# A new written order for all steps, and two kinds of rounding taken from VectorE and given to ScalarE alone

## The chip, the cores and the metric

One Trainium2 chip, one core. The metric is the device time of one execution in microseconds (us); lower is better. Engines are named as in the profile: PE is TensorE's matmul, PEld its weight load, DVE is VectorE, ACT is ScalarE, POOL is GpSimd, SP is SyncE, which here issues all DMAs.

## The reference

Attention over pooled queries, followed by a two-layer MLP, all in float32:

```python
q_pool = q.reshape(B, H, S // 2, 2, D).mean(axis=3)          # B=4, H=8, S=1152, D=64
scores = scale * np.matmul(q_pool, k.transpose(0, 1, 3, 2))
attn = np.exp(scores - scores.max(-1)) ; attn = attn / attn.sum(-1)
x = np.matmul(attn, v)  ->  [2304 tokens, 512]
h = x @ w_in                                                  # [2304, 2048]
out = np.maximum(0.01 * h, h) @ w_out                         # [2304, 512]
```

## The kernel before

The work is cut into 3557 steps. There are 32 heads (4 batches of 8) and 9 token blocks of 256 for the MLP. Each operand of a precise matmul is split into a rounded high part and the rest, its low part, and three products of the parts are summed in PSUM. For keys these are `k_hi` and `k_lo`, for queries `q_hi` and `q_lo`, for an MLP block's input `x_hi` and `x_lo`, for the activations between the layers `post` 1 and `post` 2.

A head runs through these steps. `load_k`, `load_q`, `load_v` bring its inputs; `k_tr` and `q_tr` transpose on PE; `qk` (L465, L468) computes scores once to find each row's maximum, which DVE reduces straight from PSUM (`vmax`, L480); `m_tr`, `m_cp` (ACT) and `m_dma` (two DMAs, L500) lay the negated maxima out as one row of a matmul operand, `mt`; `qkt` (L515, nine tiles t) computes the scores again, transposed and less the maximum; `exp` (ACT, L519) writes a tile to SBUF; `esum` (POOL, L529) adds tiles up; `pv` (PE, L541) multiplies by V; `r_mm` sums over keys, a short chain of small DMAs inverts that sum and spreads it, `norm` and `scale` finish the head, and `x_out` writes it to DRAM.

An MLP block i waits for the heads that it needs, then `x_load` (SP) brings its input from DRAM, `x_hi` rounds it, `x_lo` (POOL, L675) takes the rest, and `l1` (L695) multiplies by w_in tiles that `ws_load` fetches again and again (512 KB each). Blocks 0 to 3 go on with `post` 0 (ACT, L703, the leaky ReLU), `post` 1 (rounding to the high part, helper line L259), `post` 2 (POOL, L708, the low part) and `l2` (L827 to L829). Blocks 4 to 8 use a seven-product scheme for the second layer (`g_act`, `g_mix`, `g_hi`, `g_lo`, `l2s` at L786, `o_mix`). Blocks 0 to 3 are interleaved with the heads; blocks 4 to 8 come mostly after them.

What sets the order: `ORDER` is a string of 3557 characters; each character is a letter for one of 65 families of steps (`FAMILIES`, `LETTERS`), and stands for that family's next step. `Scheduler.run` goes through it and issues each step in turn, so the string fixes the order of instructions in every engine's own queue. Where a step's `eng` names two engines, the planner picks the one that by its own books finishes it first; `lock=True` marks, in these books, a step that DVE and POOL may not run at the same time. Every engine takes its queue strictly in order, so a step that waits holds back all that are written behind it on the same engine.

Of the kernel before, what the change touches and what calls it, by code (L numbers as in the profile page):

```python
# [43 lines left out]
)  # L44
LETTERS = "!#$%&()*+,-./0123456789:;<=>?@ABCDEFGHIJKLMNOPQRSTUVWXYZ[]^_`abcd"
ORDER = (
    "!@(!#$)*%(++!,+#,+,B,$---%)*...-.--...+(+A-,-/)01*.&!-++.2.-,3,34-(,4.-34#5.AA..33$4A-%B34/01.53--442.53344#)B"
    ".$(33%-.4B4--*+,6+,.33..!CDC4D4E&/E63AAB4&34B-)355805412.34-37-54.*B.+(,-+,AA!63344.#$5%3-69B.)4:-B8../3434-0."
    "-13-..55&4573!3-9;.54555-434234*3+3.44,+,7#<=:-$.#$A./B%%63F-.->.;4F96?0GG1834&-5(33.-44.<3-5&)5342553-44.=3C."
    "!C4H34.D6C*DAEFE+3>4DE#:+,,GH3$/63CF5%CD;4EFGGC344!DE7DE01(A-A<9?H.--.63.434-=2334&433!>B):44.F#*+8-;6+,.,$535"  # L50
    "553%GCH?44-384(3A.!.</B4-3-..46)0*-1-DA6E.=.(23H++,,-4-F>7.FA..934/35-)3?8-.434&34BB5554.-0-1A3.3445555G55.-#$"
    ".C7(93%-..4233:;*44++G3B3:D6A,&,/0<F4G455;<134E3-4CDF.G34)-6B!3.-.43E5#B-243$=>=>7%.455C3*4+AD3E+-4-,B9?,C6.8!"
    "C..A-FDDGE/E.36FF40-B3.(1:-H.5F73494?34;5-32U38)-&43.&-...43<4435#43:$3;45*G/345%01(3C6++,D,CEGDE=A4B6>35442A)"
    "?85345-.*++33<,,#4UA=$-.6(34A-47935.-46%>)!-?FHRF8G.34.3-../-45&5-3.S743.G(394--..T4*G5H:+B,CBV;:&<VVVVBDV0#1+"
    "C!625WED-,-55FEF6=$X.)..%/3;3U4G4G#3$%37A>0434A91A34(4-.3H344-3*?52++643,4,34.5U-65<5Y354.U:;3-H8=3.44>73CCDED"
    "E5BVVVVVVVVU4<--9FW?G.F..XC8/!DVVVVGC30WA1HH4EDE63344=-23>43.-A)343B55X.55YY?546344348-*UU#+$VU.VVV+:%,,VUVW--"
    ".-VVV.&5555VV.!V3A./0W4155X-3B3B4.#2-.YBB63F43$%CD44-E6U-GC.FF34-GDE7..93344;&-34.53.54G/3HCD05ZCDEFE4ZZFFZZZZ"
    "B5GGCZHZZZHG1XCCCDEZ[ZAVZYFG:HDDUUZEE5DFGE3F2VGZ[VUVVVVVVVVVFW43W;5(5)<<B6CDX34G4=BE*+>?,F3+,35U584643345YA473"
    "-GCVXU=>V9V(D:VEVF.ZV;ZZW?ZY4ZZ8&A3<-=G-X.YZZZZZ&)4.--..-.ZZZ!.U[>/UZZ*01+U+,,6355555[2R5#S3?4T434$%68A33-7A43"
    "4943.-.-.VVVV4-.-(.-..&UU:5VVVVVVWV3/55X)*++UU0!15VVV;55WVVV,XUYYVVVV<W4Z34#,Z$%(VXVVWAX-3-.4ZZYY-..=23-ZZZZ55"  # L60
    "[U796U34.4)>*+,&A?:334;<+555645,=3-3844-A334.>3..(/04)71?546!69823344#ZZZZ$-:;<%.5555-.-.&!ZZZA=Z-3]]5.[>55-43"
    "43*VVVV+,.V?V+-4()3WA,43..47/012343#XUU*U4++,5,555$%633449-53.63555-48U3.4-43AA.344-3-VV:VV(VVV!YVVVV.;55U-U)W"
    "...XY554<VWXYVVVVVVWXY(=>UUU/ZZZZ034ZZZ12Z6&3?[3744RST334#*9:$6]43%)-++,,;55555<=8.3-4VVVU>UVVV4Z55WZ-!-X..-VV"
    ".ZVZVV3.-4#..34VZZZZ$/&%&[0AAA?-W6.132!-.4337-4.43(Y-.6-4U8X3.9:35555544-U5533..*/04;431Y+2,3+76,4<54334#)&*=>"
    "++4AU6,,VVVVVV9$W5?8VVVVVVW3%-A3-44A:&X.334-4355554.-Z-..!-;55.ZZ.YZZX().3/05#$1Y4UUZU2!5ZZ[-3-%.465.34555-3.4"
    "<73-=.9>U-6.3-4:343445;?.<3.*4/8=0A134+2346635555+43749(3A344,>?,)A*348#+3+:,!,$V%4VVV-U.-.;-.VZZ(VWZU55-.-.VV"
    "VVA-5#$3X%5U55Y!ZV4VZ..5/--0ZWAVVVV1.UVZV342.-.<-=)>Z.[XW364-.3U4374]93344(#3*5+555$+,6,&)%75U4?:YA!98334&4--;"
    "<XY3V.V4./VZ-.0551:#3VVV2Z5WXZYZZZZZ43U;.R555-$%64[34=<>=5.-3433.4(-.]*55++,,6>4-?S3434555T&../70833A1A-2A4)63"
    "49:4.;?3-63438<44-.3-434.5.5534--*+V..(5=,+!),VVVV.VWX7>?9&33/:0;416555468233#44*(+3$%+A,AZ,ZZ4-3.<55-.VZVYVU4"
    "3--.&AZU5UUZ-43ZZ.VV4V[5-W..34555553!45#.3$/01%UVVVVV4V2673W34!#43I)I$=3>4%96XXYY34?8-5543-555..:;U3443-43*V+V"  # L70
    "VVVVWVVV5+Z,,UV.4-UUU--..LVNOZ5VXWX..YM/ZZAZZZ01ZZZ<P[55QJ2KIIPQAZZZ=ZZLZ3674-34[363.&9-4>?:3445&8.-33-..4MA34"
    "-VV;-.4.VV.5YVVWX3/0U5VV515V55NVVUVVVVUV5YWXY42JVVW36434363<KO43I447XU339=4U4>R57933YS46UT546NVZIVJVPK::;;<<U5"
    "O55?VLVVVVMZ555V=QIU^VVVV>UUVVVVUUZIPZQVV5VV?Z8ZZVVZNVVJ7LI8IO^LJMZUUUVVVVVVVVVP[ZZZZZMNZZ_KKIRUUUN^VV9UQ_`VVV"
    "V`OVVaa^IV^S_VU:bbO^PTVVVV__JI`aLUVVVUVVVI[V^_bUVVMUK;QNIVVVV`a^]VV]IJJKKbLM<LMNOO`UPPVQVVUVVVUVVVab`a_`b^UVa^"
    "^UUV==VVV>>QUV^VVVVVbV_`UVVabbb^__b`a`V^c??ccUVUcVVRVVVUbcccVVaVcSbU^UVTVV^_`aUUVVVVVVVVV^_U__UUVb`VVVVVVaVb^U"
    "UUVVddVVUU__VV`Va_Vb`VVRaVVVb^`a^VVV`bUVVVabccbcbb_cUUVVVUVVVVSccccT`UUVVV^Va_^b^`_U_a_VVVVUVVVVV_^b`a^UVVVUVV"
    "VVb`UaVUV^VVUVUbVVU`VVVVabV`U`aaVV^VVVVUVVVd_RdSbb`ab^^bbccTccccbUVVVUUVVUUc__`a`VVVVaVVVVVc^b^U^UUVVVVVUU__VV"
    "Vb___VVV`aVVV`b`VVaUUVba`aU^VVVVVV^UVVVVbVd`dbabUVVV^UVV_`UVVV_`aa^bbbcc^]c_bccUUVVVVVccd`VaVbb___`a`ab`ab^_^_"
    "^_`bab`abcd`abbbbbbbbbbbbbccccccccddd"
)  # L80
TILINGS = {"pv": 1, "r_mm": 2, "qk": 3, "qkt": 3, "k_tr": 3, "q_tr": 3, "m_tr": 3}

# [134 lines left out]
def tile_pooled_attention_moe(  # L217
# [16 lines left out]
    B, H, S, D = q.shape  # L234
# [6 lines left out]
    KC = DM // 128  # L241
    NF = DFF // 128
    NB = 256
# [466 lines left out]
    S1, S2, S3, S4, A12, A22, A11, A21 = range(8)  # L710
# [158 lines left out]
    def step(fn, *a, eng, lat=None, deps=(), order=(), takes=(), lock=False):  # L869
        sch.add((fn.__name__, *a), partial(fn, *a), eng, lat, [d for d in deps if d], [d for d in order if d], takes, lock)  # L870
# [9 lines left out]
    for hd in range(NHD):  # L880
# [93 lines left out]

    for i in range(NBLK):
        step(x_load, i, **sp(1 + (i * NB // SP != (i * NB + NB - 1) // SP), 0.524e6), deps=[("x_out", hd) for hd in needs(i)] + [("x_load", i - 1) if i else None], takes=[("xb", [("l1", i, FH - 1 if i >= FAST else NF - 1, 2)])])
        step(x_hi, i, eng={"ACT": act(KC * NB), "DVE": dve(KC * NB, 2)}, lock=True, deps=[("x_load", i)])
        step(x_lo, i, eng=pool(KC * NB, "x_lo"), lock=True, deps=[("x_hi", i)])
        fast = i >= FAST
        order = [x * FH + p for p in range(FH) for x in (1, 0)] if fast else list(range(NF))  # L980
        for at, f in enumerate(order):
            (fp, _), hf = pair(i, f), f // FH
            was = order[at - 1] if at else NF - 1 if i <= FAST else FH - 1
            prev = ("l1", i, was, 2) if at else ("l1", i - 1, was, 2) if i else None
            step(ws_load, i, f, **sp(1, 0.524e6, 0.36), deps=[("w_out_dma", f), ("w_out_dma", NF - 1) if i else None],
                 order=[("ws_load", i if at else i - 1, was) if at or i else None], takes=[("ws", [("l1", i, f, 2)], 0 if i else 1)])
# [96 lines left out]
```

## Time and profile before

| | |
|---|---|
| median of 3 runs | 915.27 us (909.39 to 915.32) |
| the profiled execution | 915.84 us, of which the span from the first to the last instruction is 914.1 us |
| PE busy | 867.9 us, 95% of the span |
| DVE, ACT, POOL busy | 511.5, 391.3, 477.8 us (56%, 43%, 52%) |
| mean granted TensorE clock | 0.986 of full speed |
| chain that ended last | PE 80%, DMA 7%, DVE 4%, ACT 3%, SP's queue 3% |

A profile row gives a line of the kernel, the engine and operation, output and input tiles, the count, and times. PE is busy in nearly the whole span; a gap on PE, and time in which PE was granted less than its full clock, are what another order of the same work could win back.

### The profile page before, as it was taken

What the parts mean: (1) busy time and instruction counts of PE and PEld (TensorE: products, weight loads), DVE (VectorE), ACT (ScalarE), POOL (GpSimd) and SP (SyncE); (2) the same over time, 40 slices, a digit from 0 to 9 for tenths busy, and PEclk for the clock granted to TensorE, in tenths of its full rate; (3) what the DMA queues carried; (4) which work ended last, traced back from release to release, by engine and by line L of the source; (5) the groups of instructions that cost most, each with busy time, mean ns of one, the idle gap of its engine ahead of it and who ended that gap; (6) DMA issues with size and microseconds to landing.
All of it is one profiled execution on the core that took longest, in us unless ns stands there. A gap on an engine that the chain in (4) does not pass through costs nothing.

```text
span 914.1 us, 19773 instructions
## 1 busy us (share of the span) xinstructions
PE 867.9 (95%) x7736; PEld 696.0 (76%) x7736; DVE 511.5 (56%) x829; ACT 391.3 (43%) x708; POOL 477.8 (52%) x382
## 2 busy tenths in 40 slices
PE   4999898999899999989999999999999999999997
PEld 2766565666678787767776777778778999999997
DVE  6777566564774443462545454365477945335354
ACT  2557464655555344343354344543432332323232
POOL 1557495675779675664868658847771101102000
PEclk9999997999999999999999999999999999999999
DMA  5656656476776563445553554354448677776740
GB/s 143 186 173 187 195 156 207 135 220 209 252 239 202 177 208 107 123 153 170 162 140 126 166 155 124 88 176 132 129 131 273 196 256 222 228 230 212 234 132 35
DMA packets 107309, 159.74 MB, mean 175 GB/s; under 512 B 25856, under 2 KB 74304, under 8 KB 107216
## 3 DMA queue, kind: packets, MB, share of 16 engines
q1 hardware_dynamic: 107216, 158.48, 56.8%
q8 instruction: 61, 1.00, 0.5%
q14 instruction: 32, 0.26, 0.1%
HBM read 131.12 MB, written 17.90 MB: 163 GB/s over the span
## 4 chain that ended last, share of the span: by engine, by line
PE 80%; DMA 7%; DVE 4%; ACT 3%; SPq 3%; issue 2%; POOL 1%; DVEq 0%; ACTq 0%; POOLq 0%
PE banks L695 22%; PE banks L515 15%; PE banks L541 13%; PE banks L786 11%; PE banks L465 4%; PE banks L827 3%; PE banks L828 3%; PE banks L829 3%; DVE stat L480 3%; DMA ws<-wd 2%; DMA mt<-ms 1%; ACT e L519 1%; PE banks L552 1%; PE banks L557 1%; PE banks L468 1%
## 5 line engine op out<-in xcount | busy, mean ns | idle before, releaser
L480 DVE TENSOR_REDUCE stat<-banks 128x1 f32<-128x1024 f32 (+3 forms) x224 | 217.2, 1006 | 100.4 <-PE banks L465 84.7
L519 ACT ACTIVATE e<-banks 128x576 f32<-128x576 f32 x232 | 146.2, 650 | 144.7 <-PE banks L515 124.4
L695 PE MATMUL banks<-xb,ws 128*128 128x256 f32 x1344 | 177.1, 287 | 3.7 <-DMA ws<-wd 3.0
L695 PEld LDWEIGHTS banks<-xb,ws 128*128 128x128 f32 x1344 | 168.4, 192 | 12.2 <-DMA ws<-wd 3.2
L515 PE MATMUL banks<-qh,ka 64*128 64x288 f32 x1152 | 146.5, 328 | 10.3 <-DVE ql L436 3.7
L529 POOL TENSOR_TENSOR sm<-sm,e 128x576 f32<-128x576 f32 x98 | 138.6, 1435 | 7.7 <-ACT e L519 7.7
L515 PEld LDWEIGHTS banks<-qh,ka 64*128 64x128 f32 x1152 | 95.3, 191 | 56.1 <-ACT e L519 17.9
L541 PE MATMUL banks<-e,vv 128*64 128x288 f32 x928 | 131.4, 415 | 0.5 <-DVE stat L480 0.4
L541 PEld LDWEIGHTS banks<-e,vv 128*64 128x64 f32 x928 | 65.0, 138 | 47.0 <-issue 7.9
L515 PE MATMUL banks<-mt,hot 64*128 64x288 f32 x576 | 91.6, 299 | 4.8 <-DMA mt<-ms 4.7
L595 POOL TENSOR_TENSOR x<-x,rs 128x288 f32<-128x288 f32 x32 | 25.7, 806 | 126.4 <-DMA rs<-rd 85.8
L515 PE MATMUL banks<-ql,ka 64*128 64x288 f32 x576 | 89.2, 297 | 0.0
L529 POOL TENSOR_TENSOR sm<-e 128x576 f32<-128x576 f32 x53 | 75.1, 1427 | 25.6 <-ACT e L519 25.6
L465 PE MATMUL banks<-ka,qh 64*128 64x512 f32 (+1 forms) x320 | 71.8, 452 | 9.6 <-DVE stat L480 5.6
L515 PEld LDWEIGHTS banks<-mt,hot 64*128 64x128 f32 x576 | 59.5, 190 | 6.5 <-DMA mt<-ms 6.4
L786 PE MATMUL banks<-wo,gg 128*128 128x256 f32 x356 | 62.4, 282 | 0.0
L515 PEld LDWEIGHTS banks<-ql,ka 64*128 64x128 f32 x576 | 58.0, 190 | 0.0
L436 DVE SCALAR_TENSOR_TENSOR ql<-banks,qh 64x288 fp32r<-64x288 f32 x66 | 29.9, 453 | 47.4 <-ACT qh L433 42.3
L708 POOL TENSOR_TENSOR gg<-g,gg 128x512 fp32r<-128x512 f32 x32 | 41.1, 1286 | 24.9 <-ACT gg L259 19.5
L827 PE MATMUL banks<-wo,gg 128*128 128x512 f32 x128 | 52.6, 411 | 0.0
L786 PEld LDWEIGHTS banks<-wo,gg 128*128 128x128 f32 x356 | 51.2, 189 | 0.0
L465 PEld LDWEIGHTS banks<-ka,qh 64*128 64x128 f32 (+1 forms) x320 | 30.8, 183 | 26.5 <-DVE stat L480 8.9
(201 smaller groups left out, 1405.4 us busy)
## 6 DMA issues: line engine op xcount, KB each, us to landing
ws<-wd SPq DMA_DIRECT2D x144, 512.0 KB
kn<-in_k_dram SPq DMA_DIRECT2D x32, 288.0 KB
qn<-in_q_dram SPq DMA_DIRECT2D x128, 72.0 KB
vv<-in_v_dram SPq DMA_DIRECT2D x32, 288.0 KB
raw<-in_moe_w_in_dram SPq DMA_DIRECT2D x16, 512.0 KB
raw<-in_moe_w_out_dram SPq DMA_DIRECT2D x16, 512.0 KB
wd<-ws SPq DMA_DIRECT2D x16, 512.0 KB
rs<-rd SPq DMA_DIRECT2D x64, 72.0 KB
```

What stands on the lines that cost most here:

```text
L436: nc.vector.scalar_tensor_tensor(out=q_half(ql[hd], x, y), in0=q_src(hd, x), scalar=QSCALE, in1=f32(q_half(qh[hd], x, x)), op0=ALU.mult, o ...
L465: nc.tensor.matmul(p[:n, x, :KW], lhsT=qh[hd][r, o:o + n], rhs=kh[r, :KW], start=True, stop=True)
L480: nc.vector.tensor_reduce(out=d, in_=p, axis=AX.X, op=ALU.max)
L515: nc.tensor.matmul(p[:, x, :HW], lhsT=w[r], rhs=m[r, hf * HW:(hf + 1) * HW], start=(n == 0), stop=(n == 3))
L519: nc.scalar.activation(out=ex[hd, u], in_=sps.pop((hd, u))[:, :, :HW], func=AF.Exp)
L529: ENG[e].tensor_tensor(out=o, in0=a, in1=b, op=ALU.add)
L541: nc.tensor.matmul(p[64 * hf:64 * hf + 64, :HW], lhsT=vv[hd][:, t, :], rhs=probs(hd, t, hf), start=(t == 0), stop=(t == KT - 1),)
L695: nc.tensor.matmul(p, lhsT=wst[i, f][:, a, c, :], rhs=xx[i][x][:, c, :], start=(n == 0), stop=(n == 3 * KC - 1))
L708: ENG[e].tensor_tensor(out=t[:, 1], in0=gf.pop((i, fp)), in1=f32(t[:, 0]), op=ALU.subtract)
L786: nc.tensor.matmul(o, lhsT=g[i, p][:, a], rhs=w[:, x], start=(p == 0 and n == 0 and half == 0), stop=(p == FH - 1 and n == 2), skip_group_ ...
L827: nc.tensor.matmul(p, lhsT=gh, rhs=wo[f][:, 0], start=(f == hf * FH), stop=False)
L828: nc.tensor.matmul(p, lhsT=gh, rhs=wo[f][:, 1], start=False, stop=False)
```

## The change

Two things. The string `ORDER` is replaced by another permutation of the same 3557 steps; and two step kinds lose the choice of DVE: `x_hi` (it also loses its `lock`) and `post` 1 now name ACT alone.

```diff
@@ ORDER (33 of its 33 lines differ; the first two of each are shown) @@
-    "!@(!#$)*%(++!,+#,+,B,$---%)*...-.--...+(+A-,-/)01*.&!-++.2.-,3,34-(,4.-34#5.AA..33$4A-%B34/01.53--442.53344#)B"
-    ".$(33%-.4B4--*+,6+,.33..!CDC4D4E&/E63AAB4&34B-)355805412.34-37-54.*B.+(,-+,AA!63344.#$5%3-69B.)4:-B8../3434-0."
...
+    "!#$%()*+!(,++#,+$,,)--%.-.B!.*-(++A@.--...--!,)/B01B*.+.--2.,+3,,3(-4344A3..-A4#.3$4-&./501%34)34-33.B.-244AB#"
+    "$33.-44334&4(%.*C!-.++6-,6DC..55DE3E3)A84-4/,013B4355B-(43..555574&-A*.+2,-+.),6339B#AF443$-F%6&-.433855-4G4.-"
...
@@ steps of an MLP block @@
-        step(x_hi, i, eng={"ACT": act(KC * NB), "DVE": dve(KC * NB, 2)}, lock=True, deps=[("x_load", i)])
+        step(x_hi, i, eng={"ACT": act(KC * NB)}, deps=[("x_load", i)])
...
-                step(post, i, fp, 1, eng={"DVE": 0.75, "ACT": act(512)}, deps=[("post", i, fp, 0)])
+                step(post, i, fp, 1, eng={"ACT": act(512)}, deps=[("post", i, fp, 0)])
```

Read out letter by letter, the two strings compare as follows. Both hold the same 1296 PE steps; the first 19 are the same, and 856 of the 1296 positions hold another step. PE changes between kinds of tiling 263 times in either. Between a head's `m_tr` and its first `qkt` stood fewer than 6 PE steps for 12 of the 32 heads, and now for 7. SP's steps right ahead of head 8's `m_dma` were `load_v` 8, `r_row` 4, `r_row` 5, `w_load` 23, `load_k` 11, `w_load` 8 (a `w_load` is 512 KB), and now are `r_row` 4, `q_dup` 9, `r_wide` 4, `r_row` 5, `load_k` 11, `q_dup` 9. On ACT's queue the three `x_hi` of blocks 2, 3 and 4 now stand right ahead of `exp` steps (head 20 tile 5, head 25 tile 8, head 31 tile 3); SP's `x_load` 4 is written directly ahead of `x_hi` 4.

## Rows read from the trace of the kernel before

**Rows 1.** Busy time per stretch: us, PE, PEld, DVE, ACT, POOL (instructions), PEclk, DMA share, GB/s
```profile
0.00:25.00 25.00, 13.39 (x81) 8.12 (x83) 17.35 (x28) 6.87 (x14) 4.53 (x13) 1.00 0.51 143
...
60.00:245.00 185.00, 170.06 (x1742) 117.69 (x1734) 120.52 (x180) 105.68 (x196) 119.61 (x96) 0.95 0.63 187
...
260.00:390.00 130.00, 128.72 (x1085) 98.15 (x1082) 63.01 (x89) 61.47 (x116) 92.24 (x73) 1.00 0.57 173
402.50:700.00 297.50, 293.15 (x2585) 225.28 (x2584) 152.70 (x219) 121.27 (x232) 198.53 (x150) 1.00 0.49 146
...
700.00:907.70 207.70, 207.68 (x1723) 206.33 (x1721) 109.75 (x257) 68.59 (x102) 18.36 (x19) 1.00 0.63 202
```

**Rows 2.** Helper line L259: engine, operation, tiles, count, duration ns min/median/max, first and last start
```profile
L259 ACT CAST gg<-g x19: 610/621/653, 232.5 to 660.6; 128x512 fp32r<-128x512 f32 x19
...
L259 DVE CAST gg<-g x13: 408/427/8407, 205.2 to 665.4; 128x512 fp32r<-128x512 f32 x13
...
L259 DVE CAST xb<-xb x5: 693/695/940, 325.4 to 833.4; 128x1024 fp32r<-128x1024 f32 x5
L259 ACT CAST xb<-xb x2: 1040/1042/1044, 194.9 to 756.1; 128x1024 fp32r<-128x1024 f32 x2
```

**Rows 3.** Timeline around 390 us, DVE, POOL and PE: start, duration, what, idle before
```profile
387.37 8.41 DVE L259 CAST gg<-g 128x512 fp32r<-128x512 f32 x1
395.70 0.91 DVE L436 SCALAR_TENSOR_TENSOR ql<-banks,qh 64x288 fp32r<-64x288 f32 x2
...
387.25 2.79 POOL L529 TENSOR_TENSOR sm<-e 128x576 f32<-128x576 f32 x2
390.00 5.50 POOL L529 TENSOR_TENSOR sm<-sm,e 128x576 f32<-128x576 f32 x4
395.57 1.47 POOL L529 TENSOR_TENSOR sm<-sm 128x576 f32<-128x576 f32 x1
...
396.67 0.53 PE L515 MATMUL banks<-qh,ka 64*128 64x288 f32 x4 [3.70 <-DVE ql L436]
```

**Rows 4.** Timeline around 245 us, DVE, POOL and PE, columns as above
```profile
240.76 7.27 DVE L259 CAST gg<-g 128x512 fp32r<-128x512 f32 x1
247.96 1.21 DVE L480 TENSOR_REDUCE stat<-banks 128x1 f32<-128x1024 f32 x1
...
242.38 4.15 POOL L529 TENSOR_TENSOR sm<-sm,e 128x576 f32<-128x576 f32 x3
...
249.22 0.50 PE L465 MATMUL banks<-ka,qh 64*128 64x512 f32 x2 [2.93 <-DVE stat L480]
```

**Rows 5.** Busy time per stretch around three PE gaps, columns as in rows 1
```profile
245.00:250.00 5.00, 2.07 (x30) 1.60 (x30) 4.77 (x4) 1.19 (x2) 4.64 (x5) 1.00 0.93 320
250.00:255.00 5.00, 5.00 (x39) 4.80 (x37) 2.63 (x4) 1.42 (x3) 4.84 (x4) 0.66 0.84 252
392.50:397.50 5.00, 1.25 (x16) 0.79 (x12) 4.92 (x4) 0.65 (x1) 4.84 (x5) 1.00 0.91 333
397.50:402.50 5.00, 4.98 (x30) 3.02 (x30) 1.23 (x1) 1.60 (x3) 3.65 (x3) 0.66 0.42 119
...
147.50:152.50 5.00, 4.23 (x34) 2.76 (x28) 2.78 (x5) 2.32 (x7) 2.82 (x3) 0.50 0.74 216
152.50:157.50 5.00, 5.00 (x23) 2.56 (x25) 4.13 (x8) 3.08 (x7) 2.63 (x2) 0.50 0.60 169
```

**Rows 6.** Busy time of two 25 us stretches, columns as in rows 1
```profile
225.00:250.00 25.00, 21.95 (x223) 16.62 (x223) 19.43 (x21) 13.70 (x25) 15.15 (x13) 1.00 0.75 238
375.00:400.00 25.00, 20.72 (x185) 15.55 (x185) 18.99 (x15) 10.22 (x19) 19.21 (x15) 0.95 0.56 178
```

**Rows 7.** Timeline at head 8's maxima: ACT's copy, SP's queue, and PE
```profile
134.45 0.26 ACT L493 CAST ms<-banks 5x128 fp32r<-5x128 f32 x1 [0.94 <-DMA rt<-rs]
...
138.99 1.60 SPq L500 DMA_DIRECT2D mt<-ms  x2
...
145.33 0.81 PE L515 MATMUL banks<-mt,hot 64*128 64x288 f32 x2 [2.03 <-DMA mt<-ms]
```

**Rows 8.** Waits over the whole span: engine, line, waited for: us in total, times, longest
```profile
PE banks L695 <- DMA ws<-wd: 3.0, 3, 1.8
...
DVE xb L259 <- DMA xb<-xd: 14.0, 4, 4.7
...
ACT xb L259 <- DMA xb<-xd: 1.8, 1, 1.8
```

More of the change, by code (lines that the diff above doesn't have):

````diff
@@ L46 @@
 ORDER = (
-    "!@(!#$)*%(++!,+#,+,B,$---%)*...-.--...+(+A-,-/)01*.&!-++.2.-,3,34-(,4.-34#5.AA..33$4A-%B34/01.53--442.53344#)B"
-    ".$(33%-.4B4--*+,6+,.33..!CDC4D4E&/E63AAB4&34B-)355805412.34-37-54.*B.+(,-+,AA!63344.#$5%3-69B.)4:-B8../3434-0."
-    "-13-..55&4573!3-9;.54555-434234*3+3.44,+,7#<=:-$.#$A./B%%63F-.->.;4F96?0GG1834&-5(33.-44.<3-5&)5342553-44.=3C."
-    "!C4H34.D6C*DAEFE+3>4DE#:+,,GH3$/63CF5%CD;4EFGGC344!DE7DE01(A-A<9?H.--.63.434-=2334&433!>B):44.F#*+8-;6+,.,$535"
-    "553%GCH?44-384(3A.!.</B4-3-..46)0*-1-DA6E.=.(23H++,,-4-F>7.FA..934/35-)3?8-.434&34BB5554.-0-1A3.3445555G55.-#$"
@@ L52 @@
[L52 to L76, printed above, removed]
@@ L77 @@
-    "VVb`UaVUV^VVUVUbVVU`VVVVabV`U`aaVV^VVVVUVVVd_RdSbb`ab^^bbccTccccbUVVVUUVVUUc__`a`VVVVaVVVVVc^b^U^UUVVVVVUU__VV"
-    "Vb___VVV`aVVV`b`VVaUUVba`aU^VVVVVV^UVVVVbVd`dbabUVVV^UVV_`UVVV_`aa^bbbcc^]c_bccUUVVVVVccd`VaVbb___`a`ab`ab^_^_"
-    "^_`bab`abcd`abbbbbbbbbbbbbccccccccddd"
+    "!#$%()*+!(,++#,+$,,)--%.-.B!.*-(++A@.--...--!,)/B01B*.+.--2.,+3,,3(-4344A3..-A4#.3$4-&./501%34)34-33.B.-244AB#"
+    "$33.-44334&4(%.*C!-.++6-,6DC..55DE3E3)A84-4/,013B4355B-(43..555574&-A*.+2,-+.),6339B#AF443$-F%6&-.433855-4G4.-"
@@ new lines @@
+    "!./0134..-7553.3!-9B(:;44.2A-33.*44+53357)4,G4<+#5H,-#$6:=$>A..%3%9-./-6.4;031-&434B?8.-A3555534H-34..2434-33C"
+    "C!..44C!6*D<3DEEFD+E/4+,&,#3(=C56$G34D%>E:3FGC;FGC4D5EBA4D70E3-1-?).59B.6!-3<.A2443345HH5-343445534.#8*+,-.63="
+    "+$>,%3(FF:4;-.B4)33.A/4-.-?8604F&.C-D1<G.-*+6,G+-,GE-79....&(=AB2334>A-4?335/484-5555.01-3B3.4-3!.44#.3-4.$739"
+    "%:HA2344-3..3;)544*5++B34(/,,3603CF4B:<A1)=3;4-5-D455>E63C<..43!GAD4#$-E.23B%475C3*=>943D++E,34?,B-4--....F/6!"
+    "8F:;FAU3-?&4GG.-60.G3C-1D&843E5555F7.34-.(394A24-343)-43&..4#$34./<*H:%34301=+;+>5,536(,CC4D<63GA?4EDE=2FF83-4"
@@ new lines @@
+    "4.)*U++,,H5354>3#-74$.3-G6%C4.34-(D6E55-5?A9834.)!35-A-....R-H4:.3SU47/93;3-4*G4TV.V-0VVVV+,BC(A<B.1+C#255D556"
+    ",FEW5$F-)%DE&3344633G4.!-..4=A/3434#>$01BG7934-%-6.33FU.55G:?4-4;8.HBC234*+5,5!65+3,DX&&434-(34553.-.U<:43V;H5"
+    "CEDE4AVVVVVW3=-U..<>7BCFAVV9VVVV/G4FDE0C?YG3=WHH1253-8>4645555.DE633A)U44-3434.-?3384#U5554-C.*.VV++DE,XUX,UVV"
+    "VVV--:Y&!$VVVYAVF.VGW..X/F3%(;WA04)-B1.33#4-6<2$4%H3-.X=B4-63..3-44334.-5.45553G374>BBBY./430CZ1DEZZZCDE9ZZFFH"
+    "YCCFZZGGGZCZZZDDEFGEFGDZZU[54HUVVVV2:CUU?EFDEG555F3VVWGBZZV4;V[VVVV555W85BBCH36X344*<+33YUU+DEF446A53=G3,,U744"
@@ new lines @@
+    "U3VXYCC4VV>DEFGZ9VVVDEZZZWXZY-F?G5!-5ZRZZZ..--8-.:&Z5;Z(Z)34.-<.S=../ZZZZ[[03*>A1++76,23T443,U4#$U353645559%A3"
+    "44?-(8535-]V]:VVVVVVVVVVVWX4!.U-..W#$-VV5XVUVYVVZ)W*.%+U+X3U,YY,4VVV;&--.(3VVV4AA<WX3A-../0&.1ZYZ=Z>U4-.&--..Z"
+    "555ZZ)2Z[6-34!3473.9*43:+6,+,43-?3;A4555543<U.54(57934.=/301>2?466U3:#483VVZ4Z8$%;V---<ZUZVVVW..X).ZZZZ-[343.4"
+    "!-.A(3*VVVY5555+U=>+4AVVVWXY),-3,3U55544555U6../01?3A34&#42*++,76,393$%-.843-434&344U.-3-45533555.4-:.VVVVVVVV"
+    "V.;A-../U4WXVV<Y(VAZ3)0ZZWX=4ZYZZZZ[U&61234373!>#44(534*$?+R,65%39-+4,8:.S!3;-<4ZZZT=.Z---A.VVZZZ.U&55#3$U.-.Z"
@@ new lines @@
+    "54[VVU)%55./VVV340A->5WVV51VV.555V3?26XW-43344YXY(7.39--4:6..34-34U8;-5334U<!45.*.5.3/05124=376)455+*++3,,9#64"
+    "&3,+>,$UAVV?VV54VVW]8354%-.34-33.4:4X-3-VYVZV4!..3-UU-;.VVAVW<XZ]=Z../Z5555#01Y455ZZZ555Z$A![34>2A--%63.-4.347"
+    "35.-.-96344.(3:?-;.3<4)4.3555/5*4(38013)=44>62655+3+,,55344793*?AU348434#+3+4VV!Z$,ZZ-%-VVV5V()W,UUZ5.--.-V:.A"
+    "..VVUVVV3&;<#W4-X35554!../$VVAUZZZ=>YV%0134--VZ.[VV-55U5.X-.6WX.23A43-74(3344.#$%*Y63-?955++,A4,!33478..-3Y/44"
+    "V:;.VVVV9&VZUU5:5-&&.W-<XY5R0ZZZZZ.ZZ12#53U$S6A[-4;%=)*34+,63.55+43,-.<>TU=4>3434-&34A.34.7?/55555-801334646(2"
@@ new lines @@
+    "3.?!9:4A5-833-4433..-;<)4433445-*+.+-=(.,5..5>,)VVV/VVVW012?A#34347$6%659:;<33844*+=-+53Z5Z4Z!5555.(-34,,-Z3.-"
+    "4VUVVV.UXZZZZ5Y-).3.4[VVW-3AA4AU3#U!.>4$X.3/014VVV2VVV6%3W3455#4$-%IU7-U..63?9-38I44-34.3-53555&.4*4:Y3.43-+,+"
+    ",VV55;VVVVVV55WXXAV5YYV.5.4VZVWXYZ/0ZZZZZ1Z5<=2>P3Q6?463L8N4-[U37U3.-49A.4:3455-.3U3M4O]-]53&-4ZJ..4ZZV&555V-V"
+    "VVVU55KW5ZZZZZ.I.VU/XYVVVV;0UUN314[2OIVW5VVLMJKXPVVVV6QY<=WXI3344734363YRS4U93N43:4473>936;T44556VUVV555V?555V"
+    "8U:;RV<VV=VVZZUZ7>9VZVU<^UIUIIPZVVVVV:VVVLOM;^LUUVUPVVZQNZJZMZK<INVVVJVVVVVVZ_ZKZIJ[LOUVVQUO?IVZZZVVU_ZIN[`]LK"
@@ new lines @@
+    "a8UPJO^VU=V^V`QPM_SaTKVV=VVVVVb`bU^U^UVVVVVVVVVVUVVQU>U_a_?`ab^VVVVVVV`>UUUU?bMIIa^JbLV__VV^VVVNVVPMKIVV`aVVNO"
+    "UUb^IJLUU^`_QKPaOQ`VVVVVVVVVVMRaSVVbbT^^bbcccb_`aUUVVVUcVccccU^VVVVUUVV_VVb`UUVVV^abVV___VVVVVV`aVb`aUUUU`^bV_"
+    "a_bVVV_V`^`V`V]VabVaVd^UVVaVVUbbccVUVVVVbbbVUR_`_a`a^^^U^cc_VVcccVVVVbbST_dVUUVVV`VVV_a_^_UVVVUVVV`bUUUdUa`^VV"
+    "VbVV^VV_VVaVVV_bcUUVVVVV```aVUUVVVUUabba^b`bVc^a^^cbVc_cbbVV`aUVVVVVVV^V^__RST`UVVbV`UUaaVVVVVVUbVV^V^_ccccUUU"
+    "VbVVVVV____VVV`aUUVVVVU`a^b`UUa^bdVVdVVb`VVa`_`UbbbbVVUUcacVcc^aVV^bVbVVVU__cccdc`a`a_`aVVVVVV^_UUb`aVVV^_V`ba"
@@ L80 @@
+    "VVVV^_d`bbabbbbbbbbcccbbcccbbbbccdddd"
 )
````

## The prediction

> **What bounds the kernel now.** I read busy time per stretch first, because the same PE work stays in both kernels: only PE gaps, and time at a lower granted clock, can be won or lost by an order. [rows 1] cut the span in five. From 700 us to the end of PE's work the gaps sum to 0.02 us of 207.70: that last stage is PE's alone, and no order gains there. In the first 25 us PE has gaps of 11.61 us, but PE's first 19 steps are the same in both strings, so they stay. What is left is the middle. From 60 to 245 us the gaps are 185.00 − 170.06 = 14.94 us, and a mean granted clock of 0.95 costs another 0.05 × 185 = 9.3 us. From 260 to 390 us there are 1.28 us of gaps, from 402.5 to 700 us 4.35 us.
>
> Then I looked between these stretches, with the timeline. Near 390 us [rows 3] a rounding of `post` 1 on DVE, a 128x512 cast, lasts 8.41 us, while the median of its 13 is 427 ns [rows 2]. In that time POOL runs six `esum` additions one right after the other (two in 2.79 us, four in 5.50 us). The cast's end, 387.37 + 8.41 = 395.78 us, falls at the seam between the sixth and the seventh. So the row shows a DVE cast that gets no turn while POOL's queue is full, and takes its turn when POOL pauses. Behind it in DVE's queue stand the `q_lo` that frees a PSUM bank and a key's low part; PE waits 3.70 us for the `q_lo`. Near 245 us [rows 4] the same happens: the cast lasts 7.27 us next to POOL's additions, a `vmax` is queued behind it, and PE waits 2.93 us for that. After each gap the clock falls: PE ran at full clock before it and idle inside it, and the 5 us after it have a mean of 0.66 [rows 5], a stretch at the lower level, 1.2 GHz, and then 2.4 GHz again.
>
> The Trainium skill's page "SBUF — State Buffer", section "Who interferes with whom", says that a DVE cast in a two-port mode and a GpSimd instruction take turns at a shared port pair, each for a whole instruction, and that ScalarE waits for nobody. By that, the first cast would have waited for one addition, about 1.4 us, and PE not at all; the trace's 8.41 us spans six additions, so here the measurement decides.
>
> **The change part by part.**
>
> *`post` 1 on ACT alone.* It removes 13 DVE casts, two of them the long ones, and adds 13 ACT casts. What PE gets back: 3.70 + 2.93 = 6.63 us of gaps, and after each (1 − 0.66) × 5 us = 1.7 us of clock [rows 3 to 5], in all 6.63 + 3.4 = 10.0 us. Bounds: above, the whole gap of both 5 us stretches, 2.93 + 3.75, and the clock, 10.1 us; below, nothing, if PE runs at once into what is next late. What is next late behind 397 us is a weight tile (`ws_load`); all three such waits of PE in the whole span sum to 3.0 us [rows 8], so I take 10.0 and keep 7.0 as the low side of this mechanism.
>
> Its cost: 13 × 0.62 us = 8.1 us more of ACT [rows 2]. What hides it is ACT's idle time: ACT is idle 11.3 us of 25 around the first place and 14.8 us of 25 around the second [rows 6], mostly waiting for PE. I price it at nothing; if the cover were gone it would be at most 8.1 us, spread over 13 places of 0.62 us. The cast stands behind `post` 0 on the same engine, so it adds no wait for another one.
>
> *`x_hi` on ACT alone.* Five DVE casts of 0.695 us (median) become ACT casts of 1.04 us [rows 2]: 5.2 us of ACT against 3.7 us of DVE or a little more. Two of nine blocks' casts already ran on ACT into the same tile. The new thing is a wait. On DVE the cast stood waiting for its input's DMA four times, 14.0 us in all, 4.7 us at most [rows 8]. On ACT, whatever is written behind it waits too: `exp` steps for blocks 2, 3 and 4, and PE has only two PSUM score buffers to run ahead with. I take 0 for it, since PE has `pv`, `l1` and `l2` work written between, and keep the full price for the rival below.
>
> [...]
>
> *The lock.* `x_hi` without it only changes the planner's books. DVE's remaining work from SBUF does not change.
>
> *The order.* PE's steps and tiling changes are the same in number, so no term comes from PE's own work. For the 24.2 us of gaps and lost clock from 60 to 245 us, and the 5.6 us of gaps after 260 us, I have no row that says how they fall anew. One place can be read. Head 8's maxima were ready on ACT at 134.71 us, but SP issued their DMA only at 138.99 us and PE waited 2.03 us for it, until 145.33 us [rows 7]. After that PE ran at the lower clock for at least the 10 us of [rows 5] with a mean of 0.50, which loses 5.0 us: some 7 us for one late row of maxima. The new string has no weight load among SP's six steps ahead of it, where there were two of 512 KB, but a `q_dup` and an `r_wide` that wait for other engines. Fewer heads have a short way from `m_tr` to the first `qkt` (7, from 12). That leans towards a gain, but other heads have more SP steps ahead of their maxima. I put the order at 0, between −7 (this place mended and no new one) and +8 (one more such place).
>
> *Sum.* The profiled execution is 915.84 us: 914.1 us of span and 1.74 us around it. 915.84 − 10.0 = 905.8 us. The median of the runs shown is 0.57 us lower, so 905 us against 915.27 us, −1.1%. About 1% is what a measurement of this kernel can tell from no change; its three runs lie 0.65% apart.
>
> **The rivals.**
>
> *A. As above: the two held casts go, the rest is redrawn to about the same.* 900 to 911 us, 905 likeliest. For it: both places are explained row by row. Against it: it assumes that 24 us of other gaps stay equal under an order that changes two thirds of PE's positions. Chance 0.45.
>
> *B. The order gives most of it back: one more late row of maxima (or a late `q_dup`), with its stretch at 1.2 GHz.* 905 + 8 = 913 us, not to be told from before. For it: a gap of 2 us cost 7 us at head 8, so one is enough. Chance 0.25.
>
> *C. The order mends head 8's place and adds none.* 905 − 7 = 898 us or somewhat less. For it: the two weight loads are gone from in front, and five heads got a longer way. Chance 0.18.
>
> *D. Slower: ACT stands at `x_hi` for its DMA with `exp` queued behind.* Per block 4.7 us of ACT at the most [rows 8]; exposed in full on PE and with 1.7 us of clock after it, 6.4 us, for blocks 2, 3 and 4 together 19.2 us: 905 + 19.2 = 924 us, and more if the low clock lasts as long as at head 8 (3 × 5.0 in place of 3 × 1.7 gives 934). It decides from about 19 us, that is, only when all three waits are nearly full. For it: `x_load` 4 is written directly ahead of `x_hi` 4, with `exp` behind. Against it: SP's queue runs by itself and issues `x_load` as soon as its slot is free, and the two `x_hi` that ACT had waited 1.8 us in all [rows 8]. Likeliest of this case 927 us; chance 0.12.
>
> **How the numbers follow.** Predicted is A's 905 us. Range: C down to 894 us (its 898 with another gap of some 4 us gone), B up to its 913 and a part of D below its decision point, 919 us; left out are most of D and the far ends of the others, together about 0.2. A's own range is 900 to 911. Faster by over 1% means below 906.1 us: all of C (0.18) and some 0.29 of A's 0.45, 0.47. Slower by over 1% means above 924.4 us: most of D and a little of B's far end, 0.12. Between: 0.41.
>
> **What would show it.** In the profile of the changed kernel L259 has no DVE cast into `gg` or `xb`, 32 ACT casts gg<-g near 0.62 us and 9 ACT casts of 128x1024 near 1.04 us; DVE's busy time falls by 8.41 + 7.27 + 11 × 0.41 + 5 × 0.69 = 23.6 us or more, ACT's rises by about 13. PE's gap total (span less busy, 914.1 − 867.9 = 46.2 us) falls by 6 or 7, and no PE wait above 2.5 us is put down to DVE. If the clock mean stays at 0.986 although those gaps are gone, B holds; if it nears 0.995, C. D shows as ACT waits for DMA xb<-xd above 3 us with PE waiting for ACT's `e` right behind. The forecast is wrong if a wait of a kind that this trace does not have takes the place, or if PE loses more at 60 to 245 us than the 24 us it loses now.

## The result, and the profile after

The changed kernel takes 884.08 us (883.7 to 884.74, 4 runs), the kernel before, beside it, 913.83 us (909.39 to 915.32, 4 runs): a ratio of 0.968, 95% interval 0.965 to 0.972. That is 30 us faster, below the range of 894 to 919 us.

Busy time per stretch of the changed kernel (columns as in [rows 1]; its PE work ends at 878.2 us):

```profile
60.00:245.00 185.00, 177.69 (x1853) 124.86 (x1851) 125.80 (x192) 113.18 (x211) 130.05 (x104) 0.97 0.66 197
260.00:390.00 130.00, 129.79 (x1097) 100.54 (x1096) 55.96 (x80) 61.65 (x113) 94.35 (x73) 1.00 0.60 178
402.50:700.00 297.50, 296.64 (x2610) 231.80 (x2607) 158.90 (x232) 128.85 (x242) 207.57 (x163) 1.00 0.53 156
700.00:878.20 178.20, 178.16 (x1509) 177.97 (x1508) 87.83 (x199) 59.19 (x85) 22.29 (x31) 1.00 0.60 196
```

Against [rows 1]: PE's gaps shrink from 14.94 to 7.31 us in the stage of the heads (60 to 245 us), from 1.28 to 0.21 us and from 4.35 to 0.86 us in the next two. The roundings, from the rows of line 259 (columns as in [rows 2]):

```profile
L259 ACT CAST gg<-g x32: 609/621/644, 211.2 to 637.6; 128x512 fp32r<-128x512 f32 x32
...
L259 ACT CAST xb<-xb x7: 1040/1044/1047, 185.2 to 816.0; 128x1024 fp32r<-128x1024 f32 x7
```

No cast is held: 644 ns is the longest, where [rows 2] had 8,407. From the waits over the whole span (columns as in [rows 8]), two rows of the changed kernel, then one of before:

```profile
ACT xb L259 <- DMA xb<-xd: 1.6, 3, 1.1
PE banks L515 <- DMA mt<-ms: 1.6, 4, 0.4
```
```profile
PE banks L515 <- DMA mt<-ms: 4.7, 6, 2.0
```

ACT has taken over all `x_hi` (seven into `xb`; the other two go into `ka`, on ACT before too), and stands 1.6 us for the loads of `xb`; on DVE it was 14.0 us [rows 8]. The chain of work that ended last, by engine, before and then after:

```profile
PE 80%; DMA 7%; DVE 4%; ACT 3%; SPq 3%; issue 2%; POOL 1%; DVEq 0%; ACTq 0%; POOLq 0%
```
```profile
PE 87%; DMA 5%; POOL 2%; ACT 2%; DVE 2%; issue 1%; SPq 1%; POOLq 0%; ACTq 0%; DVEq 0%
```

**Where 31.5 us of span went** (914.1 to 882.6 us, profiled executions, PE's own accounts). PE's gaps, span less busy: 46.2 to 24.8 us, −21.4. By stretch: −0.9 up to 60 us, −7.6 from 60 to 245, −6.3 at the two held casts (245 to 260 and 390 to 402.5 us), −4.6 in the two stretches from 260 and 402.5 us, −1.9 behind PE's last matmul. PE's busy time: 867.9 to 857.8 us, −10.1. Of these, time at 1.2 GHz before 870 us falls from 23.9 to 10.2 us, half of which is lost, so −6.9; and the 1,728 `l1` matmuls follow one another 117.8 ns apart in place of 119.2, so −2.4. The profiled executions are no accident in this: the mean clock is 0.993 to 1.000 in the four runs of the changed kernel, and 0.981 to 0.994 in the runs of the kernel before beside the experiments.

**What else moved.** Where a step may run on either of two engines, the planner chose anew under the new string. Worked out from the two kernels, 37 steps beside the 18 casts changed engine: 18 of the weight sums and of the later blocks' `g_mix` and `g_lo` went from DVE to POOL and 3 back, 8 `norm` from ACT to DVE and 4 back, 4 others. The traces show it: POOL has 415 instructions where it had 382 and is busy 500.1 us where it was 477.8, and DVE runs 19 of the 32 `norm` copies where it ran 15. Every "new order" below includes these moves, and no run separates them from the order itself.

### The profile page after: what moved, and what is told of

The parts are those of the page before. It is cut to its first block, busy times and chain, and to the rows that moved or that the text cites. A ratio compares the mean times of both kernels' runs of the same rounds, so it can differ in the third digit from the quotient of the medians.

```text
span 882.6 us, 19778 instructions
## 1 busy us (share of the span) xinstructions
PE 857.8 (97%) x7736; PEld 687.3 (78%) x7736; DVE 483.1 (55%) x780; ACT 403.2 (46%) x724; POOL 500.1 (57%) x415
## 4 chain that ended last, share of the span: by engine, by line
PE 87%; DMA 5%; POOL 2%; ACT 2%; DVE 2%; issue 1%; SPq 1%; POOLq 0%; ACTq 0%; DVEq 0%
PE banks L695 24%; PE banks L515 18%; PE banks L541 14%; PE banks L786 11%; PE banks L465 5%; PE banks L827 4%; PE banks L828 3%; PE banks L829 3%; PE banks L552 1%; DMA qh<-qh 1%; PE banks L557 1%; DVE stat L480 1%; POOL sm L529 1%; ACT e L519 1%; DMA qn<-in_q_dram 1%
## 5 line engine op out<-in xcount | busy, mean ns | idle before, releaser
L519 ACT ACTIVATE e<-banks 128x576 f32<-128x576 f32 x231 | 146.0, 651 | 141.7 <-PE banks L515 121.9
L695 PE MATMUL banks<-xb,ws 128*128 128x256 f32 x1344 | 174.2, 284 | 0.1
L695 PEld LDWEIGHTS banks<-xb,ws 128*128 128x128 f32 x1344 | 164.8, 189 | 9.2 <-issue 3.6
L529 POOL TENSOR_TENSOR sm<-sm,e 128x576 f32<-128x576 f32 x96 | 134.8, 1429 | 4.2 <-ACT e L519 4.2
L515 PEld LDWEIGHTS banks<-qh,ka 64*128 64x128 f32 x1152 | 92.5, 189 | 49.1 <-issue 16.9
L515 PE MATMUL banks<-mt,hot 64*128 64x288 f32 x576 | 89.7, 296 | 1.7 <-DMA mt<-ms 1.6
L529 POOL TENSOR_TENSOR sm<-e 128x576 f32<-128x576 f32 x53 | 74.7, 1425 | 24.8 <-ACT e L519 24.8
L515 PEld LDWEIGHTS banks<-mt,hot 64*128 64x128 f32 x576 | 57.6, 187 | 3.3 <-DMA mt<-ms 3.2
L675 POOL TENSOR_TENSOR xb<-xb 128x1024 fp32r<-128x1024 f32 x7 | 16.7, 2387 | 66.0 <-ACT xb L259 66.0
L827 PE MATMUL banks<-wo,gg 128*128 128x512 f32 x128 | 52.1, 407 | 0.0
L415 POOL TENSOR_TENSOR qs<-qn 112x384 f32<-112x384 f32 x32 | 32.1, 1005 | 33.2 <-DMA qn<-in_q_dram 28.0
L828 PE MATMUL banks<-wo,gg 128*128 128x512 f32 x128 | 50.5, 394 | 0.0
```

What stands on the lines that cost most here:

```text
L415: ENG[e].tensor_tensor(out=qs[hd][:n], in0=a, in1=b, op=ALU.add)
L515: nc.tensor.matmul(p[:, x, :HW], lhsT=w[r], rhs=m[r, hf * HW:(hf + 1) * HW], start=(n == 0), stop=(n == 3))
L519: nc.scalar.activation(out=ex[hd, u], in_=sps.pop((hd, u))[:, :, :HW], func=AF.Exp)
L529: ENG[e].tensor_tensor(out=o, in0=a, in1=b, op=ALU.add)
L695: nc.tensor.matmul(p, lhsT=wst[i, f][:, a, c, :], rhs=xx[i][x][:, c, :], start=(n == 0), stop=(n == 3 * KC - 1))
L827: nc.tensor.matmul(p, lhsT=gh, rhs=wo[f][:, 0], start=(f == hf * FH), stop=False)
```

## The experiments

All ran beside the kernel before, in groups; its median was 909.4 to 915.2 us from group to group, so a difference between kernels of two groups is good to a few us, and the ratio to the kernel before beside it is the safer number. "All on ACT" means both edits of the change (`post` 1 and `x_hi` on ACT alone); in the first four runs the engine is set where the step is issued, so all other choices of the planner stay those of the string's own kernel. Pairs like (0, 2) are a block and a pair of its column groups; `l2s` 8.7.3 is block 8, pair 7, part 3, and `o_mix` 8.2 is block 8, combination 2.

### Order and engines taken apart

```diff
 # old_order_act: kernel before, both roundings on ACT    (old_order_two_act: only `post` 1 of (0,2) and (1,4))
     def post(...)
+            e = "ACT"                       # two_act: e = "ACT" if (i, fp) in ((0, 2), (1, 4)) else e
     def x_hi(i, e):
+        e = "ACT"                           # two_act: without this
 # new_order_same_dve: changed kernel, the 13 + 5 casts that DVE had before are put back
+            e = "DVE" if (i, fp) in (the 13 of before) else "ACT"
+        e = "DVE" if i in (1, 2, 3, 4, 8) else "ACT"
 # new_order_all_dve: changed kernel, all 32 `post` 1 on DVE
+            e = "DVE"
```

> The old order, with all 32 post 1 casts and all 9 x_hi casts on ScalarE; the planner's other choices stay as they were. Theory of the prediction (two held casts cost 10 us, the order does the rest): 904 us, ratio 0.989. Rival 1, the casts are the whole gain: 884 us, ratio 0.967. Rival 2, the casts are only where a loss shows that returns elsewhere at once: 911 us or more, ratio 0.997 or more.

> The old order with only the two held casts (block 0 pair 2, block 1 pair 4) on ScalarE. Theory: all that the move to ScalarE gives in this order is those two, so 904 us, within 2 us of the run with all casts moved. Rival, holds move on to the next cast on VectorE: less than half of the gain, 909 us or more.

> The new order with the same 13 post 1 casts and 5 x_hi casts on VectorE that the kernel before had there. Theory: a cast is held only where GpSimd's queue is full beside it, and which ones meet that changes with the order: between 884 us (none held) and 894 us (two held). Rival, the new order has room for any held cast: 884 to 886 us.

> The new order with all 32 post 1 casts on VectorE: the suspected cost, more than doubled. Theory: two of 13 were held for 7 to 8 us and cost 5 us each; of 32 some five are, 884 + 25 = 909 us, and casts of several us show in the profile with GpSimd's additions beside them. Rival, held casts hide in the new order: below 890 us.

| kernel | us, median (runs from to) | ratio to before, 95% |
|---|---|---|
| old order, all on ACT | 910.63 (907.48 to 915.78) | 1.000 (0.997 to 1.002) |
| old order, two casts on ACT | 902.03 (899.28 to 905.49) | 0.990 (0.986 to 0.993) |
| new order, the same casts on DVE | 885.87 (882.76 to 887.62) | 0.971 (0.968 to 0.975) |
| new order, all `post` 1 on DVE | 892.0 (890.61 to 893.35) | 0.978 (0.976 to 0.981) |

What follows, with 912.03 us for the kernel before beside these four: the two casts alone are worth 912.03 − 902.03 = 10.0 us in the old order, the forecast's 10. The order with the planner's other moves is worth 912.03 − 885.87 = 26 us. The moved casts on top of it give 1.8 us by the medians, and the two ratios' intervals overlap. The two gains are not a sum: the new order takes most of the held casts' cost away by itself (of its 13 + 5 casts on DVE only one `post` 1 and one `x_hi` last over 2 us, 5.04 and 2.42 us). With all 32 `post` 1 on DVE it loses 8 us, between the 25 us and the at most 6 us that were expected; two casts are held, 4.82 and 5.27 us, where five were expected. Moving the other 11 casts and `x_hi` as well costs the old order 8.6 us. Where, its timeline shows (start, duration, what, idle before):

```profile
310.73 1.55 SPq L500 DMA_DIRECT2D mt<-ms  x2
...
312.38 0.39 SPq L667 DMA_DIRECT2D xb<-xd  x1
...
316.27 1.04 ACT L259 CAST xb<-xb 128x1024 fp32r<-128x1024 f32 x1 [4.83 <-DMA xb<-xd]
...
317.34 0.65 ACT L519 ACTIVATE kn<-banks 128x576 f32<-128x576 f32 x1
...
318.04 0.85 PE L515 MATMUL banks<-qh,ka 64*128 64x288 f32 x4 [3.88 <-ACT kn L519]
```

The load of block 1 (counted from 0; L667) is queued behind head 16's maxima (L500), for which SP stands until 310.73 us. ACT stands 4.83 us at the rounding, an `exp` (L519) waits behind it, PE waits 3.88 us, and 6.8 us at 1.2 GHz follow. This is rival D, at its full price in one place and not three; at block 2 ACT stands 1.46 us and PE 1.62 us.

In the new order the one long-held `post` 1 also costs less. DVE, POOL and PE around 430 us, new order with the same casts on DVE:

```profile
424.12 5.55 POOL L529 TENSOR_TENSOR sm<-sm,e 128x576 f32<-128x576 f32 x4
...
426.15 5.04 DVE L259 CAST gg<-g 128x512 fp32r<-128x512 f32 x1 [1.96 <-ACT g L704]
...
429.63 1.27 POOL L710 TENSOR_TENSOR gg<-g,gg 128x512 fp32r<-128x512 f32 x1
...
431.11 1.21 DVE L480 TENSOR_REDUCE stat<-banks 128x1 f32<-128x1024 f32 x1
...
432.38 0.73 PE L465 MATMUL banks<-ka,qh 64*128 64x512 f32 x4 [1.24 <-DVE stat L480]
```

5.04 us of hold become 1.24 us of PE; in [rows 3, 4] 8.41 and 7.27 us became 3.70 and 2.93.

### The late load: the wrong block, then the right one

```diff
 # in ORDER, on top of old_order_act
-...x_load 2, x_load 3 where they were         # old_order_act_early_load
+...each right behind the last l1 of the block before it
-...m_dma 16, x_load 1                         # old_order_act_load1
+...x_load 1 19 steps earlier, behind ws_load (1, 1), ahead of m_dma 16
```

> The old order with all casts on ScalarE, and x_load of blocks 2 and 3 moved in SP's queue to where their slot comes free (behind the last l1 of the block before). Theory: the run with all casts on ScalarE gained nothing because ScalarE stood at these two x_hi for their DMA, with exp queued behind (PE waits of 3.88 us and 1.62 us, and 6.8 us at half clock behind the first); without that wait it gains what the two held casts cost: 902 us, ratio 0.989. Rival, 13 us more work on ScalarE is what costs: still 908 us or more.

Measured: 911.49 us (907.95 to 919.02), ratio 1.000 (0.998 to 1.003): a miss, and by a mistake of counting. Blocks 2 and 3 were moved; the wait of 4.9 us belongs to block 1, and stayed, with 3.95 us of PE at 321.94 us.

> The old order with all casts on ScalarE, and the load of activation block 1 (the second) issued 20 steps earlier, ahead of the maxima's transfer of head 16 at which SyncE stands for 6 us. In the old order with all casts on ScalarE that load starts at 312.4 us, ScalarE then stands 4.83 us at the block's rounding with an exponential behind it, and TensorE 3.88 us, 6.8 us of clock at half speed after it. (The earlier try moved blocks 2 and 3, and left this one.) Theory (the loss is the load queued behind a standing transfer): both waits go, 3.9 + 3.4 = 7 us less than the 910.6 us of that kernel, 903 to 904 us. Rival (old order gives it back at the next late step): 908 us or more.

Measured: 904.45 us (900.32 to 908.54), ratio 0.993 (0.991 to 0.995), 6.2 us less than old_order_act. Its timeline:

```profile
307.02 0.42 SPq L667 DMA_DIRECT2D xb<-xd  x1
...
313.59 1.55 SPq L500 DMA_DIRECT2D mt<-ms  x2
...
314.32 1.05 ACT L259 CAST xb<-xb 128x1024 fp32r<-128x1024 f32 x1
```

SP still stands for the maxima, but the load is past it, and ACT does not wait. The new order has the load written 48 steps ahead of these maxima; it goes at 291.08 us, the rounding at 300.43 us. From 25 to 700 us SP stands some 65 us at L500 in the kernel before and some 29 us in the changed one (sums of the rows of SP's waits, the largest of before and of after):

```profile
SPq L500 <- ACT e L519: 19.8, 5, 7.3
...
SPq L500 <- ACT ms L493: 17.3, 6, 4.9
```
```profile
SPq L500 <- ACT ms L493: 7.6, 8, 2.0
...
SPq L500 <- ACT e L519: 6.7, 8, 2.8
```

### The tail

```diff
 # in ORDER, on top of old_order_two_act
-l2s 8.7.0 ... l2s 8.7.6, o_mix 8.0 to 8.7
+... l2s 8.7.3, o_mix 8.0 to 8.2, l2s 8.6.4, l2s 8.7.4, o_mix 8.3 to 8.5, ... l2s 8.7.6, o_mix 8.6, 8.7
```

> The old order with only casts (0,2) and (1,4) on ScalarE, and the last block's eight combinations written between its last second-layer matmuls, as the new order has them, in place of behind all of them. Theory: VectorE starts them while TensorE still works, and what follows TensorE's last matmul shrinks by 1.9 us: 900 us against the 902.0 us of that kernel; the time alone can't carry that, so the stretch from TensorE's end to the last transfer in the trace decides. Rival: TensorE waits for VectorE instead, and the stretch shrinks while TensorE ends later.

Measured: 899.35 us (895.6 to 902.27), ratio 0.987 (0.983 to 0.991). The last rows of PE, DVE and SP, in the kernel before and then with the edit:

```profile
907.45 0.28 PE L786 MATMUL banks<-wo,gg 128*128 128x256 f32 x1
...
907.76 2.33 DVE L806 TENSOR_TENSOR raw<-raw,banks 128x256 f32<-128x256 f32 x6 [0.23 <-PE banks L786]
...
910.11 1.30 SPq L818 DMA_DIRECT2D out_dram<-raw  x3
```
```profile
894.69 1.21 DVE L807 TENSOR_TENSOR raw<-raw,banks 128x256 f32<-128x256 f32 x3 [0.28 <-PE banks L787]
...
895.78 0.28 PE L787 MATMUL banks<-wo,gg 128*128 128x256 f32 x1
...
896.10 0.42 DVE L807 TENSOR_TENSOR raw<-raw,banks 128x256 f32<-128x256 f32 x1 [0.20 <-PE banks L787]
...
896.55 1.31 SPq L819 DMA_DIRECT2D out_dram<-raw  x3
```

Written behind all `l2s`, six combinations run after PE's last matmul; written between them, one does. SP's output transfers follow PE's end by 2.38 us before, by 0.49 us with the edit: 1.9 us, as expected. The changed kernel has the same tail.

### The addresses of the buffers

A buffer gets its place in SBUF at its first use, so another order is another layout.

```diff
 # new_order_old_layout: changed kernel, all buffers allocated first, in the old order's sequence
 # new_order_apart: the same with xb ahead of x1, rs, rt and with ws 0, 1 behind them
+    for t in ("kn:0 kn:1 ka:0 ...").split():
+        o, i = t.split(":")
+        sb.tile([128, 2 * DM] if o == "wo" else spec[o][1], F32 if o == "wo" else spec[o][2], tag=o + i, name=o)
```

> The changed kernel with one thing altered: every SBUF buffer lies at the address that it has in the kernel before (buffers are laid out in the order of their first use, so the written order moves them). No step, queue or engine is altered. In the traces so far the first-layer matmuls (128x256, line 695) follow one another 119.2 ns apart in the kernel before and 117.8 ns in the changed one. Theory (the spacing goes with the addresses of the activation block and of the four weight buffers): 119.2 ns, so 1728 x 1.4 ns = 2.4 us more, 886.5 us. Rival (the spacing goes with the order itself, with what the other engines do meanwhile): 117.8 ns and 884.1 us.

> The changed kernel with three buffers moved: the activation block xb lies in front of the small ones, weight buffers 0 and 1 behind them, so that address of block minus address of weights, modulo 256 bytes, is 64 for all pairs, and never 0 as it is for about half of the first-layer matmuls of the changed kernel. In its trace pairs with 0 follow 119 to 120 ns apart, pairs with 64 some 115.7 ns, all together 117.8. Theory (address pairs set the spacing): about 115.8 ns, 1728 x 2.0 = 3.5 us less, 880.6 us. Rival (in the trace of the kernel before such pairs stand at 117.8 ns): no gain, 884 us.

Measured on one chip: old layout 886.50 us (884.85 to 887.53), apart 882.13 us (881.06 to 883.5). Mean distance from start to start of `l1` matmuls that follow one another, worked out from all their start times in the traces, by block address minus weight address, modulo 256 bytes (addresses worked out from the sequence of allocation; spread over pairs of buffers):

| kernel | all | difference 0 | 64 | 192 |
|---|---|---|---|---|
| before | 119.2 ns | 119.6 | 117.8 | |
| changed | 117.8 | 119 to 120 | 115.2 to 116.2 | 116.0 to 117.1 |
| new order, old layout | 119.0 | 119.3 to 119.9 | 117.2 to 117.8 | |
| new order, apart | 117.4 | | 117.1 to 117.5 | |

The old addresses bring most of the old distance back with nothing else altered, so 1.2 to 1.4 ns × 1728 = 2.1 to 2.4 us of the result are layout. Apart wins 4.4 us over the old layout, of which the distance gives 1.7 ns × 1728 = 2.9. Against the changed kernel it is not settled: 882.13 is below 884.08 us, but the ratios to before are equal (0.968 each). Of the 3.5 us forecast the distance gave only 0.4 ns × 1728 = 0.8, since its pairs at 64 run at 117.4 ns and not at 115.7: the difference modulo 256 alone does not set the distance. What else does is open.

### Halves exchanged

```diff
 # new_then_old: the new string up to the first qkt of head 16 (about 255 us), the rest in the old string's order; all on ACT
 # old_then_new: the reverse
```

> All casts on ScalarE; the new order up to the first qkt of head 16 (some 255 us), the old order from there. If the order's gain lies where PE's gaps were (7 us of gaps before 255 us, the x_hi waits, some 4 us of smaller gaps, 2 us of the end and a slower l1 after it), this is 884 + 15 = 899 us, and the two hybrids' excesses over the new kernel add up to that of the old order with all casts on ScalarE, 27 us. Rival, an order is worth something only as a whole: both hybrids above 905 us.

> All casts on ScalarE; the old order up to the first qkt of head 16, the new order from there. By PE's gaps the first 255 us of the old order cost 7 to 10 us more than those of the new one: 892 us. Rival as for the other hybrid: above 905 us.

Measured: 897.95 us (896.47 to 901.65) and 903.78 us (901.08 to 906.35). So the new order's second part is worth 13.9 us and its first 19.7; the sum, 33.6, is more than the 26.5 us between 910.63 and 884.08. Whether the parts lean on each other is not shown: the 7 us are no more than the spread of what eight traces with the old order up to 245 us lose there (18.4 to 25.6 us, see below). old_then_new missed its 892 by 12 us, for two reasons that its trace shows. What it lost between 60 and 245 us (gaps and half of the time at 1.2 GHz) was 25.6 us, where old_order_act, with the same steps up to there, lost 18.8. And block 1's load still stands right behind head 16's maxima, since the new string moves it in its first part:

```profile
317.47 1.55 SPq L500 DMA_DIRECT2D mt<-ms  x2
...
319.12 0.39 SPq L667 DMA_DIRECT2D xb<-xd  x1
...
322.92 1.04 ACT L259 CAST xb<-xb 128x1024 fp32r<-128x1024 f32 x1 [4.74 <-DMA xb<-xd]
...
324.69 0.85 PE L515 MATMUL banks<-qh,ka 64*128 64x288 f32 x4 [3.04 <-ACT kn L519]
```

With the 6.8 us at 1.2 GHz that follow this is 6.4 us, the loss of old_order_act once more.

### Single places of the head stage

```diff
 # old_order_two_act_mt4_8: maxima of heads 4 and 8 ahead of load_v 5 / w_load 23, load_k 11, w_load 8
 # new_order_mt_on_act, old_order_act_load1_mt_on_act: maxima issued by ACT, right behind m_cp where the buffers allow
-            nc.sync.dma_start(out=f32(mt[hd])...
+            nc.scalar.dma_start(out=f32(mt[hd])...
 # *_fewer: one transfer in place of two
+        nc.sync.dma_start(out=rss[hd], in_=rd[hd].rearrange("f (o n) -> f o n", o=1).to_broadcast([2, 64, HW]))
+        nc.sync.dma_start(out=xd[b][h * D:(h + 1) * D].rearrange("d (f n) -> f d n", f=2), in_=x)
 # new_order_extra_issue, in x_out
+        nc.sync.dma_start(out=spare[hd], in_=ident[0:1])
```

> The old order with the two held casts on ScalarE, and the maxima's DMA of heads 4 and 8 moved in SP's queue ahead of the big loads directly before it (load_v 5; w_load 23, load_k 11, w_load 8). Theory: PE's waits of 1.19 and 1.62 us for these two rows go, and 6.8 us at half clock behind the second with them, so 6 us less than without the move: 896 us. Rival, late rows have other causes or the gap moves on: 900 us or more.

Measured: 907.63 us (903.0 to 911.66), 5.6 us slower than without the move by the medians, 4 us by the ratios to before (0.994 against 0.990). PE's waits for `mt` at 78 and 144 us are gone; in their place stand 1.06 us for `qh`'s transfer at 91.32 and 1.58 us for a row-sum copy at 150.81 us, and a wait for a `vmax` at 107.15 us is 2.49 us where it was 1.82. Mending head 8's place, rival C's mechanism, brings nothing by itself.

> The changed kernel with the maxima's transfers (mt, line 500, two for each head) issued from ScalarE's queue, each right behind the copy that makes their source where the buffers allow it, and no longer from SyncE's. In the trace of the changed kernel SyncE issues transfers for 86.8 of the 90 us from 60 to 150 us and 82.5 of the 95 us from 150 to 245 us; a head's two take 1.55 us of it. Theory (in the stage of the heads TensorE loses its 7 us of idle time, and the 3 us of half clock behind it, to SyncE's full queue): about half of that comes back, 879 us, and the waits for mt and qh shrink in 60 to 245 us. Rival (the next late step is as late, ScalarE's exponentials above all, which then have 1.5 us of issuing in front of them in each head): 884 us or more.

> The same edit on the old order with all casts on ScalarE and block 1's load early (904.45 us, between 900 and 908.5). There SyncE issues for 80 of the 90 us from 60 to 150 us and 87 of the 95 us behind them, and from 250 to 700 us it stands some 50 us in all at the maxima's transfers (15 us in the changed kernel), with other transfers behind them. Theory (the old order's remaining loss is in the order of SyncE's queue): the old order gains more than the new one, 10 us or more, to 894 us or less, and the two orders come to within 10 us of each other. Rival (what is late is spread over all engines): 901 us or more, and the two orders stay 17 us apart or more.

Measured: 915.15 us (912.06 to 917.71) and 912.64 us (909.53 to 914.89), so 31 and 8 us slower, where gains were expected. ACT around one such place:

```profile
123.32 0.26 ACT L493 CAST ms<-banks 5x128 fp32r<-5x128 f32 x1 [0.99 <-PE banks L489]
...
124.17 1.44 ACTq L500 DMA_DIRECT2D mt<-ms  x2
...
125.66 0.41 ACT L433 ACTIVATE qh<-banks 64x288 fp32r<-64x288 f32 x1 [2.09 <-DMA mt<-ms]
```

Here ACT is kept 2.09 us from its next step; over the 32 heads that step starts 1.57 us behind the copy in the median, where it was 0.29. SP got freer (71 of the 90 us from 60 to 150 us go to rows of issues, where it was 83 and not the expectation's 86.8) and the time rose: lateness on ACT costs more here than SP's freedom gives. Against this lateness the new order has no more room than the old; it loses all its lead, and the two orders come to within 3 us of each other.

> The changed kernel with the block's transfer to DRAM (lines 601) and the row scales' transfer back (588) issued as one transfer each in place of two: the same bytes to the same places, and 2 of the about 15 issues of a head fewer on SyncE, which spends 14.2 + 13.3 us on these lines between 60 and 245 us, so half of it, 13.7 us, goes, and nothing is added to another engine. (The last try freed more of SyncE, but put 2 us in front of ScalarE's exponentials in each head.) Theory (SyncE's queue holds up the heads in the stage of 60 to 245 us): 4 us less or more, 880 us. Rival (SyncE's queue is full but not what ends last): 883 to 886 us.

> The same edit on the old order with all casts on ScalarE and block 1's load early (904.45 us). Theory (the old order loses more to SyncE's queue than the new one): 8 us less or more, 896 us. Rival: 901 to 908 us.

> The same edit on the changed kernel with block and weights at addresses apart (882.13 us). If both gains hold and add up: 878 us; if fewer issues bring nothing: 882 us.

Measured: 964.55, 993.95 and 965.69 us (spreads of 6 to 8 us), 80 to 90 us slower, which no theory expected. Scale rows in the changed kernel, then folded:

```profile
65.38 1.19 SPq L588 DMA_DIRECT2D rs<-rd  x2
...
68.83 0.80 POOL L595 TENSOR_TENSOR x<-x,rs 128x288 f32<-128x288 f32 x1 [2.80 <-DMA rs<-rd]
```
```profile
100.97 0.57 SPq L587 DMA_DIRECT2D rs<-rd  x1
...
108.31 0.81 POOL L594 TENSOR_TENSOR x<-x,rs 128x288 f32<-128x288 f32 x1 [1.14 <-DMA rs<-rd]
```

POOL goes on as the rows land: 2.8 us after the start of the second issue at the least over the 32 heads as two transfers, 5.9 us as one. The Trainium skill's page "DMA: Bandwidth & Descriptors", section "Rules for kernel authors", has a reason why such a fold can be slow: an outermost dimension below 16 in the access patterns confines a transfer to at most that many of the 16 DMA engines, and here it is 2. The longer times agree; on how many engines it ran, no row here shows. The same section advises one 128-partition transfer in place of two halves; with 2 outermost on the DRAM side, these runs show the opposite. So they tell nothing of SP's queue.

> The changed kernel with one transfer more in each head on SyncE's queue: 512 bytes of a constant to a DRAM place that nothing reads, behind line 601's two, with nothing to wait for. It costs SyncE some 0.5 us of issuing in each head, about 6 us from 60 to 245 us, where the changed kernel's SyncE issues for 169 of the 185 us, and hardly any bandwidth. (Folding transfers told of something else: one transfer of 144 KB in place of two of 72 KB takes 5.9 us to land and not 2.8 us, and this lateness cost 80 us.) Theory (in the stage of the heads SyncE's queue is what TensorE ends up waiting for): 4 us or more added, 888 us or more. Rival (SyncE's queue has room enough at the places that matter): 886 us or less.

Measured: 886.02 us (883.57 to 888.1), ratio 0.973 (0.971 to 0.976), against 0.968 (0.965 to 0.972) of the changed kernel: 2 us by the medians, 4 by the ratios, whose intervals overlap. It falls between the two expectations and decides little: 32 × 0.43 = 14 us of issuing more on SP bring 4 us at the most, and in the stage of the heads the loss is 13.2 us where it was 12.4. That speaks against SP's queue as what this stage hangs on; it does not rule it out.

## Why the prediction was right and wrong

**The two held casts: right.** 10.0 us were forecast; the two casts alone gave 10.0 in the old order, and with them gone PE's waits for DVE at 249 and 397 us are gone.

**`x_hi` at nothing: wrong for the old order, right for the new.** Rival D's mechanism was named and priced at 6.4 us for a block. It occurs at that size once, at block 1, which the prediction had not listed, and taking it away gave 6.2 us. What the prediction did not see is that it came with a load queued behind a standing transfer, and that the new string undoes this in the same edit.

**The last stage and PE's own work at nothing: wrong, by little.** From PE's 0.02 us of gaps after 700 us the prediction drew that no order gains there, and from equal steps that no term comes from PE's own work. Two things were not in those rows: what follows PE's last matmul (−1.9 us), and how fast PE's own matmuls follow one another (−2.1 to −2.4 us by the new layout, over the whole kernel).

**The order at nothing: this is the step that failed.** Its bounds, −7 and +8, were drawn from one place, head 8. The new order, with the engines that the planner chose under it, gave −26 us with the casts where they were, and −26.5 with all on ACT. Of the latter the runs show 6.2 (block 1's load), 1.9 (tail) and 2.1 to 2.4 (layout). The other 16 us are located in part, and their cause stays open. About half lies in the stage of the heads, which the prediction named with its 24 us. There the loss (gaps and half of the time at 1.2 GHz) is 18.4 to 25.6 us in eight traces that have the old order up to 245 us, 21.3 in the mean, and 10.7 to 14.6 in seven that have the new one, 13.0 in the mean (those with folded transfers and with maxima on ACT left out). Of the 8.3 us between the means 4.2 are clock and 4.1 gaps. By what ended PE's waits there, means of the eight and of the seven: DVE 5.3 and 1.7 us (`vmax` 2.5 and 0.6, a `norm` copy 2.3 and 0.6), the maxima's transfer 4.4 and 2.6, ACT's `exp` 2.9 and 2.2, POOL's sum of query rows 0 and 2.0. A second place are the gaps from 402.5 to 700 us, 2.0 to 5.6 us in eight traces with the old order there and 0.9 in the changed kernel. So the prediction looked at one of several kinds of wait, and the largest fall is in another, the waits for DVE, whose share of the `norm` copies the planner changed too. No run altered that by itself: mending head 8's place, giving the maxima to ACT and folding transfers all raised the time, the last two by a cost of their own, and adding to SP's queue cost 4 us at the most.

**Rivals.** B (given back) did not occur. C had the sign, and the clock near 0.995 that was to show it, but its 898 us is 14 us above the result and its mechanism, one mended place, failed when tried. A held for the two casts alone, in the old order: 902 us, inside its 900 to 911.

**What was to show it.** DVE's busy time fell by 28.4 us (23.6 or more was said; the planner's other moves are in it), ACT's rose by 11.9 (13), no PE wait above 2.5 us is put down to DVE, the clock mean is 0.993. PE's gap total fell by 21.4 us where 6 or 7 was said: this sign missed, and with it the time.

## What to carry to other kernels

When two programs have the same steps and only their order differs, a trace of one gives the price of the waits that are in it, not of those that the other would have: bound an order's effect by all the idle time and lost clock of the stages that it rewrites, here 46.2 − 11.6 us of gaps and 12 us of clock, and not by the one place that can be read. Where a planner picks engines, list which steps change engine with the order, and fix them in one run. Before a step is moved onto an in-order queue, look up what is queued behind it and what the transfer that it waits for is itself queued behind. Freeing one queue at the cost of another is tested by its own run: 1.4 us of issuing in each head moved from SP to ACT cost 31 us.

## What the hardware showed that was not expected

- The distance of back-to-back 128x256 matmuls changes with where the buffers lie: 119 to 120 ns where moving block and weights have equal addresses modulo 256 bytes, 115 to 118 ns otherwise, and the old addresses in the new order bring 119.0 back from 117.8 ns. The Trainium skill's page "SBUF — State Buffer", section "Who interferes with whom", gives TensorE one read port for the moving operand and an independent one for weight loads. By that, one would not expect the addresses to matter; the measurement says otherwise, and why is open.
- With one transfer of 144 KB with a dimension of 2 outermost, POOL's next step starts 5.9 us after the start of the issue at the least; with two of 72 KB, 2.8 us after the start of the second.
- A DVE cast waits through a run of POOL's operations in the new order too (5.04 us, beside four additions and a `post` 2), so this is no accident of the old one.
